# Order of the work in a slot of a fused attention and FFN kernel: P's copy and remainder first, its third block in slot 0, the last output sums in slot 3

## The chip, the core and the metric

The kernel runs on one core of a Trainium2 chip. TensorE (PE in the profile) does the matmuls, VectorE (DVE) and ScalarE (ACT) everything on elements, SyncE (SP) issues the DMAs. The metric is the device time of one execution in microseconds (us). The kernel before takes 700.49 us, the median of three runs (700.48 to 700.79).

## The reference

Eight batches of 576 tokens and 8 heads of 64 pass through an attention over 32 landmarks for each head, and the result through an FFN without bias:

```python
a = softmax(phi, axis=2)                              # 576 x 32 for each head
k_m, v_m = einsum(a, k), einsum(a, v)                 # 32 x 64 for each head
attn = softmax(q @ k_m.T / 8)                         # 576 x 32 for each head
x = (attn @ v_m).reshape(tokens, 512)
g = silu(x @ w_in)                                    # 2048 wide
out = g @ w_out                                       # 512 wide
```

All in fp32; the kernel must return the 4608 x 512 output.

## The kernel before

**Algebra.** `x @ w_in` is never formed from x: `p_mm` (line 627) multiplies v_m with w_in, which gives P (8 heads x 32 landmarks, by 2048 columns of the FFN), and `ffn1s` (line 806) multiplies attn with P. Each large matmul works on numbers that are split into a high part in a rounded type and a remainder, so three products stand for one: high x high, high x low, low x high. The names with `hi` and `lo` are these parts.

**P.** P of a batch is made in four blocks of 512 columns. A block is 16 small matmuls into the pair of PSUM banks `bg` (there is one such pair), then a copy to the high part on ACT (line 643) and the remainder on DVE (line 645, which reads `bg` and the copy). The next block can write `bg` only when line 645 is through. Blocks 0 and 1 of batch n are made in slots 13 and 14 of batch n-1, blocks 2 and 3 in slots 1 and 2 of batch n. The piece of w_in for a block is loaded anew for each batch (`win_load`, 1 MB each).

**A slot.** Batches 2 to 7 are worked in 16 slots each: t (0 or 1, half of the tokens) by j (8 groups of 256 FFN columns). A slot is written in this order: `ffn1s` makes h (12 matmuls into the one pair of banks `h`); `forms` takes SiLU of it on ACT (line 820, and line 822 for 32 columns that are kept for later), forms differences on DVE (lines 825, 828, 829) and splits the seven operands of a Winograd step into high (ACT, lines 824 and 834) and low parts (DVE, lines 835 and 836); then come the slot's *events*; then `st_step` multiplies the seven operands of the slot before with w_out (line 845, 21 matmuls into four PSUM banks `sum0` to `sum3`). In two slots of a batch (`exp_slots`) DVE makes the last four high parts instead (lines 831, 832).

**Events** are the attention of the next batches, cut into pieces and put into slots by a table (`ev(b, slot, function, arguments)`): `p_mm`; `phi_sub` (lines 310 and 313, twice each, which subtract the maxima from phi before its exp); `s_norm` (line 442), `s_back` (transposes on DVE, line 457, then a copy on ACT, line 458) and `s_low` (line 463) of the softmax of the scores; `phi_fold` (lines 284, 286, 294, 301, 302, with small DMAs between them); loads.

**Outputs.** After slots 7 and 15 the four banks hold a finished half. `st_out` copies two banks on ACT (line 878, twice), does four additions on DVE that read the other two banks (line 885), and stores two pieces; `rest`, three more additions on line 885 and two stores, is put into the list `late`, which the next slot runs ahead of its events. The next `st_step` with j = 0 writes the four banks again.

**Left-over tokens.** 64 tokens of each batch don't fit the slots. After the odd batches there are four more slots (16 to 19, "left slots") in which those of two batches go through `left_split` (ACT line 910, DVE line 911) and `left_st` (line 845, tiles `lsum`).

**What sets the order.** PE and ACT run in the order in which the code is written (`in_order`). DVE's order is set by a scheduler from priorities; `behind(i, other)` forbids it to place i ahead of `other`. In slots 0 to 15 every DVE instruction of an event (that of `s_all` excepted) is behind the last low part that `forms` wrote (`last_split`); in the left slots there is no such rule. All engines then run their queues strictly in the order that came out.

Of the kernel before, what the change touches and what calls it, by code (L numbers as in the profile page):

```python
# [16 lines left out]
ALU = mybir.AluOpType  # L17
# [8 lines left out]
NFC = DFF // P  # L26
CW = 256
JW = 512
# [20 lines left out]
def attn_ffn_kernel(  # L49
# [9 lines left out]
    nc = tc.nc  # L59
# [60 lines left out]
    raws, cvas, last_silu, last_split = {}, {}, [], []  # L120
# [480 lines left out]

    pj, wins = {}, {}
    win_saved = [hbm.tile([P, 4, NR, P], F32, name=f"win_saved{k}") for k in range(4)]

    def win_save():
# [31 lines left out]
    def p_split(b, f, w, bg, steps=(0, 1)):  # L639
        hi, lo = pj[b, f // JW]  # L640
        c = slice(f % JW, f % JW + w)
        if 0 in steps:
            nc.scalar.activation(hi[:, :, c], bg[:, :, :w], AF.Copy)
        if 1 in steps:
            nc.vector.tensor_tensor(lo[:, :, c], bg[:, :, :w], hi[:, :, c], op=ALU.subtract)  # L645

# [220 lines left out]
        if j == NP - 1:  # L869
            st_out(b, t)  # L870

    late = []

    def st_out(b, t):
        o = sb.tile([P, 2, DMODEL], F32, tag="cva", name="oo", bufs=1)
        x = sb.tile([P, 2, Q], F32, tag="cva1", name="x", bufs=1)
        for i in range(2):
            nc.scalar.activation(o[:, i], sums[i], AF.Copy)
        (c11, c21), (p3, p5) = ((o[:, i, :Q], o[:, i, Q:]) for i in range(2))
        c12, c22 = x[:, 0], x[:, 1]  # L880
        r = b * S + 2 * t * P
        one, two = slice(r + P, r + 2 * P), slice(r, r + P)

        def add(to, a, c, op=ALU.add):
            nc.vector.tensor_tensor(to, a, c, op=op)

        add(c12, sums[2][:, :Q], c11)
        add(c22, sums[2][:, Q:], c12)
        add(c11, c11, c21)
        add(c21, c22, sums[3][:, :Q], ALU.subtract)  # L890
        nc.sync.dma_start(out[one, :Q], c11)
        nc.sync.dma_start(out[two, :Q], c21)

        def rest():
            add(c22, c22, p5)
            add(c12, c12, p5)
            add(c12, c12, p3)
            nc.sync.dma_start(out[two, Q:], c22)
            nc.sync.dma_start(out[one, Q:], c12)

        late.append(rest)

    def left_split(b, n):
        flat = gparts.rearrange("p k n f -> p (k n f)")
        home = (aparts[:, 0, 1], flat, flat[:, 2 * MAIN :], aparts[:, 1, 1])[n]
        g = gleft[:, n * NI : (n + 1) * NI].rearrange("p c f -> p (c f)")
        gs = home[:, :MAIN], home[:, MAIN : 2 * MAIN]
        if b == 1:
            return split(g, gs=gs if n == 3 else None)
        nc.scalar.activation(gs[0], g, AF.Copy)  # L910
        nc.vector.tensor_tensor(gs[1], g, gs[0], op=ALU.subtract)
        return gs

    def left_st(b, n, gs):
# [23 lines left out]
    events = {}  # L938

    def ev(b, slot, fn, *a):  # L940
        events.setdefault((b, slot), []).append((fn, a))
# [39 lines left out]
    for b in range(B):  # L981
        n = b + 1
        if b == 0:
            for j in range(2, DFF // CW):
                ev(b, 2 * j - 1.5, p_mm, b, j * CW, CW)
        elif b == 1:
            ev(b, 0, win_save)
            for j in range(1, NJ):
                ev(b, 4 * j - 3, p_mm, b, j * JW, JW)
            for j in range(NP):  # L990
                ev(b, 1.5 * j + 2, w_forms, j, 0)
                ev(b, 1.5 * j + 2.5, w_forms, j, 1)
        else:
            ev(b, 0, win_load, b, 3)
            ev(b, 1, p_mm, b, 2 * JW, JW)
            if b > 2:
                ev(b, 3, s_norm, b, SECOND)
                ev(b, 4, s_back, b, SECOND)
                ev(b, 4, s_low, b, SECOND)
            ev(b, 2, p_mm, b, 3 * JW, JW)  # L1000
            if n < B:
                steady(b, n)
            continue
# [56 lines left out]
    with in_order(DVE, ACT) as last:  # L1060
# [56 lines left out]
        bg = p_mm(0, 0, CW, False)  # L1117
# [48 lines left out]
    def finish(tiles):  # L1166
# [10 lines left out]
        elif prev[0] == "st" and tiles[0] == 0:  # L1177
            st_step(*prev[1:])

    for b in range(B):  # L1180
        if b == 1:
            whole.close()
            ctx.enter_context(in_order(ACT))
        for s in range(NFC if b > 1 else 0):
            t, j = divmod(s, NP)
            h = ffn1s(b, t, j)
            part = forms(b, t, j, h)
            todo = [(fn, ()) for fn in late] + events.pop((b, s), [])
            late.clear()
            for fn, a in todo:  # L1190
                traced = nc.cur_bb.bb.instructions
                n = len(traced)
                fn(*a)
                for i in list(nc.cur_bb.bb.instructions)[n:]:
                    if i.engine == DVE and fn is not s_all:
                        behind(i, last_split[-1])
            finish(range(NI))
            prev = ("st", b, t, j, part)
        for fc in range(NFC if b < 2 else 0):
# [23 lines left out]
        if b % 2:  # L1223
            for n in range(NLS):
                gs = left_split(b, n)
                for fn, a in [(fn, ()) for fn in late] + events.pop((b, NFC + n), []):
                    fn(*a)
                late.clear()
                finish((0, 1, 2, 3))
                prev = ("left", b, n, gs)  # L1230
    finish((0,))
# [55 lines left out]
```

## Time and profile before

| | us |
|---|---|
| median of three runs | 700.49 |
| the profiled execution | 701.35 |
| its span, first to last instruction | 699.5 |
| DVE busy | 513.8 |
| ACT busy | 367.8 |

Batches 0 and 1, which go another way and are not touched, end at about 200 us of the span; batch 2 begins its slots at 200.6, batch 3 at 280.2, batch 4 at 370.6, batch 5 at 446.3, batch 6 at 536.5 and batch 7 at 612.1 us. A slot without events takes 4.1 us, one with a block of P 5.3 us.

A row of the timeline gives the start in us, the duration in us, the engine, the line, the operation, output<-inputs, the shape and the count, and in brackets how long the engine sat idle before it and what ended that. A row of the waits gives the engine and line that waited, what it waited for, the total in us, how often, and the longest. A row of the windows gives for a stretch its length and the busy time of PE, of its weight loads (PEld), DVE, ACT and POOL with their counts, then the granted TensorE clock (1.00 is full) and the DMA share.

### The profile page before, as it was taken

The page shows a single profiled execution, that of the slowest core. Times are in us where ns is not written, and L with a number is a line of the kernel's source. Part 1 is how long each engine was busy: PE and PEld are TensorE (multiplying, and loading weights), DVE is VectorE, ACT ScalarE, POOL GpSimd, SP SyncE. Part 2 cuts the span into 40 slices and gives each one's busy share as a digit, 9 for nine tenths or more (in the row PEclk, how much of TensorE's full clock was granted, in tenths as well). Part 3 has the DMA queues.
Part 4 walks back from the last instruction along what each step waited for, and adds up shares of the span by engine and source line. Part 5 has one row for each costly group of instructions (what it writes and reads, how often), then busy time and mean ns, then how long its engine had stood idle before and what let it go on. Part 6 is the DMA issues. An engine that isn't in the chain of part 4 may idle for free.

```text
span 699.5 us, 14791 instructions
## 1 busy us (share of the span) xinstructions
PE 677.5 (97%) x5932; PEld 596.8 (85%) x5932; DVE 513.8 (73%) x1084; ACT 367.8 (53%) x676; POOL 0.7 (0%) x6
## 2 busy tenths in 40 slices
PE   7999999999999998899999999989999999999997
PEld 3578777887889997799988999889989899889996
DVE  4898799788938588858874678876885567776652
ACT  3879684543535454554644546553653645554441
POOL 0000000000000000000000000000000000000000
PEclk9999999999999999999999999999999999999999
DMA  9997974324360462243420345225431204210001
GB/s 342 340 339 264 319 280 175 111 83 159 115 191 4 169 219 66 87 163 134 156 91 17 133 134 184 77 77 179 151 105 48 77 2 147 82 75 1 31 1 46
DMA packets 37749, 93.93 MB, mean 134 GB/s; under 512 B 4657, under 2 KB 21169, under 8 KB 34097
## 3 DMA queue, kind: packets, MB, share of 16 engines
q1 hardware_dynamic: 36736, 90.22, 37.4%
q10 hardware_dynamic: 944, 2.77, 1.0%
q8 instruction: 47, 0.77, 0.4%
q14 instruction: 22, 0.17, 0.1%
HBM read 77.22 MB, written 15.73 MB: 133 GB/s over the span
## 4 chain that ended last, share of the span: by engine, by line
PE 71%; DVE 8%; ACT 5%; issue 2%; DVEq 0%; ACTq 0%
PE sum L845 29%; PE h L806 18%; PE acc L705 7%; PE lsum L845 5%; PE h L664 4%; PE bg L627 3%; DVE pm L645 2%; PE accleft L705 2%; PE bg L333 1%; ACT aparts L834 1%; ACT gbuf L820 1%; DVE gbuf L825 1%; ACT L820 1%; ACT L432 1%; PE bg L380 1%
## 5 line engine op out<-in xcount | busy, mean ns | idle before, releaser
L806 PE MATMUL h<-aparts,pm 128*128 128x288 f32 x1152 | 168.9, 295 | 0.0
L806 PEld LDWEIGHTS h<-aparts,pm 128*128 128x128 f32 x1152 | 157.0, 188 | 1.0 <-issue 0.7
L820 ACT ACTIVATE gbuf<-h 128x512 f32<-128x512 f32 x96 | 57.2, 596 | 133.7 <-PE h L806 133.4
L825 DVE TENSOR_TENSOR gbuf<-gbuf 128x256 f32<-128x256 f32 x96 | 40.4, 421 | 94.3 <-ACT gbuf L820 93.8
L845 PE MATMUL sum<-wo_hi,aparts 128*128 128x256 f32 x384 | 105.1, 296 | 1.9 <-ACT aparts L834 1.8
L845 PE MATMUL sum<-wo_lo,aparts 128*128 128x256 f32 x384 | 100.4, 283 | 0.0
L845 PE MATMUL sum<-kept,aparts 128*128 128x256 f32 x576 | 100.3, 283 | 0.0
L845 PEld LDWEIGHTS sum<-wo_hi,aparts 128*128 128x128 f32 x384 | 73.1, 190 | 24.3 <-ACT gleft L822 14.2
L834 ACT ACTIVATE aparts<-gbuf 128x512 fp32r<-128x512 f32 x86 | 54.4, 633 | 67.0 <-DVE gbuf L829 67.0
L705 PE MATMUL acc<-wo_hi,gparts 128*128 128x512 f32 x256 | 86.5, 397 | 0.3 <-DVE gparts L681 0.2
L845 PEld LDWEIGHTS sum<-kept,aparts 128*128 128x128 f32 x576 | 82.8, 191 | 0.0
L845 PEld LDWEIGHTS sum<-wo_lo,aparts 128*128 128x128 f32 x384 | 73.5, 191 | 0.0
L845 PE MATMUL sum<-wo_hi,gparts 128*128 128x256 f32 x384 | 72.7, 281 | 0.0
L836 DVE TENSOR_TENSOR gparts<-gbuf,aparts 128x512 fp32r<-128x512 f32 x86 | 59.3, 690 | 18.0 <-ACT aparts L834 18.0
L845 PE MATMUL sum<-kept,gparts 128*128 128x256 f32 x288 | 65.5, 282 | 0.0
L705 PEld LDWEIGHTS acc<-wo_hi,gparts 128*128 128x128 f32 x256 | 47.7, 188 | 14.5 <-DVE t L788 1.7
L845 PEld LDWEIGHTS sum<-wo_hi,gparts 128*128 128x128 f32 x384 | 59.4, 190 | 0.0
L664 PEld LDWEIGHTS h<-aparts,pm 128*128 128x128 f32 x372 | 51.8, 188 | 7.7 <-issue 2.7
L664 PE MATMUL h<-aparts,pm 128*128 128x288 f32 x372 | 56.2, 299 | 1.3 <-DVE aparts L463 1.0
L705 PE MATMUL acc<-wo_lo,gparts 128*128 128x512 f32 x128 | 50.5, 394 | 0.8 <-DVE wo_lo L182 0.7
L824 ACT ACTIVATE aparts<-gbuf 128x384 fp32r<-128x384 f32 x96 | 50.4, 525 | 0.0
L845 PEld LDWEIGHTS sum<-kept,gparts 128*128 128x128 f32 x288 | 47.9, 190 | 0.0
(204 smaller groups left out, 986.7 us busy)
## 6 DMA issues: line engine op xcount, KB each, us to landing
win<-win_saved SPq DMA_DIRECT2D x24, 1024.0 KB, 5.0
kv<-in_kv SPq DMA_DIRECT2D x28, 516.0 KB, 4.8
q<-in_q SPq DMA_DIRECT2D x16, 576.0 KB, 5.8
raw<-in_w_in SPq DMA_DIRECT2D x14, 512.0 KB, 7.2
raw<-in_w_out SPq DMA_DIRECT2D x6, 1024.0 KB, 5.8
win_saved<-win SPq DMA_DIRECT2D x4, 1024.0 KB, 8.7
phi<-in_phi SPq DMA_DIRECT2D x7, 576.0 KB, 6.0
out<-oo SPq DMA_DIRECT2D x26, 128.0 KB, 1.8
```

The costliest lines, as they stand in the source:

```text
L333: nc.tensor.matmul(pt[p][M * r : M * (r + 1), :KVW], e[:, p, c, M * r : M * (r + 1)], kvt[c][:, p, r], start=c == 0, stop=False, skip_grou ...
L627: nc.tensor.matmul(bg[M * r : M * (r + 1), p, :w].rearrange("p (k f) -> p k f", f=P), kvT[D * p : D * (p + 1), 1, r], src[D * p : D * (p + ...
L645: nc.vector.tensor_tensor(lo[:, :, c], bg[:, :, :w], hi[:, :, c], op=ALU.subtract)
L664: nc.tensor.matmul(h[:, hf, :HALF], wt[:, p, fs], a[:, p, hf * HALF : (hf + 1) * HALF], start=n[hf] == 0, stop=n[hf] == 5, skip_group_chec ...
L705: nc.tensor.matmul(acc[key], gt[:, cs], wt[:, fc], start=fc == 0 and n == 0, stop=fc == NFC - 1 and n == 2)
L806: nc.tensor.matmul(h[:, i, :HALF], wt[:, p, f : f + P], a[:, p], start=n == 0, stop=n == 5)
L820: nc.scalar.activation(gbuf[:, :MAIN].rearrange("p (i f) -> p i f", i=2), h[:, :, :w], AF.Silu)
L824: nc.scalar.activation(hi[:, :3], g[:, 1:4], AF.Copy)
L825: nc.vector.tensor_tensor(g[:, 4:6], g[:, :1].broadcast_to([P, 2, P]), g[:, 1:3], op=ALU.subtract)
L834: nc.scalar.activation(hi[:, 3:], g[:, 4:], AF.Copy)
L836: last_split.append(nc.vector.tensor_tensor(lo[:, 3:], g[:, 4:], hi[:, 3:], op=ALU.subtract))
L845: nc.tensor.matmul(sums[bank][:, place * Q : (place + 1) * Q], gt[:, k], wt, start=bank not in begun, stop=True, skip_group_check=True,)
```

## The change

It moves work and removes or adds none:

- `run` runs the events of a slot with `p_mm` ahead of all others, and every DVE instruction of the others is kept behind the remainder of P (line 645) of that slot.
- Block 2 of P moves from slot 1 to slot 0, for batches 3 to 7.
- `rest` is now an event. For the first half it stays in slot 9, after the others. For the second half it moves to slot 3 of the next batch from slot 1 (even batches), and stays in left slot 17 after an odd one, behind `phi_sub`.
- In the left slots DVE work of events is behind the remainder of the left-over split (line 911).

```diff
-    pj, wins = {}, {}
+    pj, wins, last_p = {}, {}, []
...
         if 1 in steps:
-            nc.vector.tensor_tensor(lo[:, :, c], bg[:, :, :w], hi[:, :, c], op=ALU.subtract)
+            i = nc.vector.tensor_tensor(lo[:, :, c], bg[:, :, :w], hi[:, :, c], op=ALU.subtract)
+            last_p[:] = [i]
...
-        late.append(rest)
+        ev(*((b, 9) if t == 0 else (b, NFC + 1) if b % 2 else (b + 1, 3)), rest)
...
-        nc.vector.tensor_tensor(gs[1], g, gs[0], op=ALU.subtract)
+        last_split.append(nc.vector.tensor_tensor(gs[1], g, gs[0], op=ALU.subtract))
...
             ev(b, 0, win_load, b, 3)
-            ev(b, 1, p_mm, b, 2 * JW, JW)
+            ev(b, 0 if b > 2 else 1, p_mm, b, 2 * JW, JW)
...
+    def run(b, slot):
+        todo = events.pop((b, slot), [])
+        todo.sort(key=lambda e: e[0] is not p_mm)
+        last_p.clear()
+        for fn, a in todo:
+            n = len(nc.cur_bb.bb.instructions)
+            fn(*a)
+            for i in list(nc.cur_bb.bb.instructions)[n:]:
+                if i.engine == DVE and fn not in (p_mm, s_all):
+                    for other in [last_split[-1]] + last_p:
+                        behind(i, other)
+
...
-            todo = [(fn, ()) for fn in late] + events.pop((b, s), [])
-            late.clear()
-            for fn, a in todo:
-                traced = nc.cur_bb.bb.instructions
-                n = len(traced)
-                fn(*a)
-                for i in list(nc.cur_bb.bb.instructions)[n:]:
-                    if i.engine == DVE and fn is not s_all:
-                        behind(i, last_split[-1])
+            run(b, s)
...
-                for fn, a in [(fn, ()) for fn in late] + events.pop((b, NFC + n), []):
-                    fn(*a)
-                late.clear()
+                if b > 1:
+                    run(b, NFC + n)
```

The new lines shift the numbers: from `p_split` to `st_out` a line after is one higher than before (836 is 837), from `st_out` on one lower (885 is 884); 627, 643, 645 and all below keep theirs. The text goes by the numbers of before.

**DVE, start of batch 3.** Before, the last row of `forms` in slot 1 (line 836) is followed by `rest`, by `phi_sub` and only then by P's remainder:

```order
L836 TENSOR_TENSOR gparts<-gbuf,aparts 128x512
L885 TENSOR_TENSOR x<-x,oo 128x256 x2
L310 TENSOR_TENSOR phi_2477<-phi_2477,am 128x512
L885 TENSOR_TENSOR x<-x,oo 128x256
L313 TENSOR_TENSOR phi_2477<-phi_2477,am 64x128
L310 TENSOR_TENSOR phi_2477<-phi_2477,am 128x512
L313 TENSOR_TENSOR phi_2477<-phi_2477,am 64x128
L645 TENSOR_TENSOR pm<-bg,pm 128x1024
```

After the change the remainder stands in slot 0, directly behind `forms` and ahead of the four additions that read the banks:

```order
L837 TENSOR_TENSOR gparts<-gbuf,aparts 128x512
L645 TENSOR_TENSOR pm<-bg,pm 128x1024
L884 TENSOR_TENSOR x<-sum_2620,oo 128x256
L884 TENSOR_TENSOR x<-sum_2620,x 128x256
L884 TENSOR_TENSOR oo<-oo 128x256
L884 TENSOR_TENSOR oo<-x,sum_2621 128x256
L826 TENSOR_TENSOR gbuf<-gbuf 128x256
```

The remainder has moved up a slot; `phi_sub` alone is left in slot 1, and `rest` stands behind line 442 in slot 3. Batches 5 and 7 begin alike (7 has no `phi_sub`). At the start of batches 4 and 6, after left slots, the remainder stands ahead of the two additions of the left-over sums (lines 932, 933).

**DVE, slots 13 to 15 of batch 3.** Before, from the last row of `forms` in slot 13:

```order
L836 TENSOR_TENSOR gparts<-gbuf,aparts 128x512
L442 TENSOR_TENSOR sc_3415<-sc_3415,ssm 128x2x288
L645 TENSOR_TENSOR pm<-bg,pm 128x1024
L301 COPY wide<-fm 128x256
L825 TENSOR_TENSOR gbuf<-gbuf 128x256
L302 STREAM_TRANSPOSE am<-wide 128x256
L828 TENSOR_TENSOR gbuf<-gbuf 128x128
L310 TENSOR_TENSOR phi_3321<-phi_3321,am 128x512
L829 TENSOR_TENSOR gbuf<-gbuf 128x128
L835 TENSOR_TENSOR gparts<-gbuf,aparts 128x384
L313 TENSOR_TENSOR phi_3321<-phi_3321,am 64x128
L310 TENSOR_TENSOR phi_3321<-phi_3321,am 128x512
```

After the change:

```order
L837 TENSOR_TENSOR gparts<-gbuf,aparts 128x512
L645 TENSOR_TENSOR pm<-bg,pm 128x1024
L442 TENSOR_TENSOR sc_3415<-sc_3415,ssm 128x2x288
L301 COPY wide<-fm 128x256
L826 TENSOR_TENSOR gbuf<-gbuf 128x256
L302 STREAM_TRANSPOSE am<-wide 128x256
L829 TENSOR_TENSOR gbuf<-gbuf 128x128
L830 TENSOR_TENSOR gbuf<-gbuf 128x128
L836 TENSOR_TENSOR gparts<-gbuf,aparts 128x384
L837 TENSOR_TENSOR gparts<-gbuf,aparts 128x512
L645 TENSOR_TENSOR pm<-bg,pm 128x1024
L457 STREAM_TRANSPOSE aT_3827<-sc_3415 128x288 x2
```

Remainder and line 442 change places in slot 13; in slot 14 the remainder goes ahead of lines 457 and 463, and `phi_sub`, which the scheduler had drawn up from left slot 17 into slot 14, goes back there. Batch 5 is the same. In batches 2, 4 and 6 the remainder moves up in slots 13 and 14 alike, without a `phi_sub`.

**ACT, slot 14 of batch 3.** Before, from `forms` of slot 14 to that of slot 15:

```order
L824 ACTIVATE aparts<-gbuf 128x384
L834 ACTIVATE aparts<-gbuf 128x512
L458 ACTIVATE aparts<-aT_3815 128x2x288
L643 ACTIVATE pm<-bg 128x1024
L820 ACTIVATE gbuf<-h 128x512
```

After the change:

```order
L825 ACTIVATE aparts<-gbuf 128x384
L835 ACTIVATE aparts<-gbuf 128x512
L643 ACTIVATE pm<-bg 128x1024
L458 ACTIVATE aparts<-aT_3827 128x2x288
L821 ACTIVATE gbuf<-h 128x512
```

P's copy goes ahead of line 458, which waits for the transposes on line 457; the SiLU of slot 15 stands behind both. PE's order changes only in that block 2's 16 matmuls stand one slot earlier; on SP the two stores of `rest` go behind one load of q in slot 9 of batch 2, and behind two of kv at the start of batches 3 and 5.

More of the change, by code (lines that the diff above doesn't have):

```diff
@@ L870, in st_step @@
             st_out(b, t)
-    late = []
     def st_out(b, t):
```

## The prediction

> **What bounds the kernel now.** First the page: its span and the busy times.
>
> ```profile
> span 699.5 us, 14791 instructions
> ...
> PE 677.5 (97%) x5932; PEld 596.8 (85%) x5932; DVE 513.8 (73%) x1084; ACT 367.8 (53%) x676; POOL 0.7 (0%) x6
> ```
>
> TensorE is busy for 97% of the span. The change removes no matmul, so it can only win what TensorE waits or runs slowly. The waits of its weight loads from 200 to 700 us, where the changed slots lie, name the causes:
>
> ```profile
> PEld sum L845 <- ACT gleft L822: 14.2, 20, 0.8
> PEld bg L627 <- DVE pm L645: 8.6, 7, 2.5
> ...
> PEld sum L845 <- ACT aparts L834: 2.2, 2, 1.1
> ```
>
> The first row is the weight loads of the sums standing still while a block of P with its small weights passes: 20 times alike, and the matmuls beside them run on. The blocks stay as many, so it stays. The second is P's block waiting until the remainder of the block before has freed `bg`; the third is the sums of slot 15 waiting for their high part. In the timeline of TensorE's matmuls these waits stand one by one:
>
> ```profile
> 270.92 1.91 PE L627 MATMUL bg<-win,kvT 64*32 64x512 f32 x16 [2.28 <-DVE pm L645]
> 293.21 1.09 PE L627 MATMUL bg<-win,kvT 64*32 64x512 f32 x16 [1.88 <-DVE pm L645]
> 349.82 1.09 PE L627 MATMUL bg<-win,kvT 64*32 64x512 f32 x16 [0.27 <-DVE pm L645]
> 359.71 0.39 PE L845 MATMUL sum<-wo_hi,aparts 128*128 128x256 f32 x1 [0.88 <-ACT aparts L834]
> 438.60 0.66 PE L627 MATMUL bg<-win,kvT 64*32 64x512 f32 x8 [0.26 <-DVE pm L645]
> 459.31 0.66 PE L627 MATMUL bg<-win,kvT 64*32 64x512 f32 x8 [1.88 <-DVE pm L645]
> 515.90 0.66 PE L627 MATMUL bg<-win,kvT 64*32 64x512 f32 x8 [0.26 <-DVE pm L645]
> 525.57 0.39 PE L845 MATMUL sum<-wo_hi,aparts 128*128 128x256 f32 x1 [0.88 <-ACT aparts L834]
> 604.34 0.66 PE L627 MATMUL bg<-win,kvT 64*32 64x512 f32 x8 [0.16 <-DVE pm L645]
> ```
>
> The brackets sum to 8.75 us. They are slot 14 of batches 2 to 6, slot 2 of batches 3 and 5, and the first left slot behind batches 3 and 5. The longest has a tail, which the windows around it show (granted clock: third number from the end):
>
> ```profile
> 267.65:271.06 3.41, 1.13 (x16) 0.90 (x22) 3.18 (x6) 2.58 (x5) 0.00 (x0) 1.00 0.00 0
> ```
>
> **The change, part by part.**
>
> *Slot 2 of batches 3 and 5.* What held `bg`, in batch 3:
>
> ```profile
> 288.37 1.01 ACT L643 ACTIVATE pm<-bg 128x1024 fp32r<-128x1024 f32 x1
> ...
> 289.11 0.75 DVE L885 TENSOR_TENSOR x<-x,oo 128x256 f32<-128x256 f32 x2
> ...
> 291.93 1.22 DVE L645 TENSOR_TENSOR pm<-bg,pm 128x1024 fp32r<-128x1024 f32 x1
> ```
>
> The copy was done at 289.38, but the remainder started at 291.93, behind `rest` and `phi_sub`. Now block 2 and its remainder lie in slot 0 and `bg` is free a slot early. What can be late next is the four banks: slot 1's sums write them again, and the additions that read them now stand behind the remainder. Slot 0 and 1 as they were:
>
> ```profile
> 283.75 0.63 ACT L834 ACTIVATE aparts<-gbuf 128x512 fp32r<-128x512 f32 x1 [0.59 <-DVE gbuf L829]
> 284.29 1.06 ACT L878 ACTIVATE oo<-sum 128x512 f32<-128x512 f32 x2
> ...
> 285.03 0.42 DVE L885 TENSOR_TENSOR x<-sum,oo 128x256 f32<-128x256 f32 x1
> ...
> 286.27 0.42 DVE L885 TENSOR_TENSOR oo<-x,sum 128x256 f32<-128x256 f32 x1
> ...
> 287.00 0.39 PE L845 MATMUL sum<-wo_hi,aparts 128*128 128x256 f32 x1
> ...
> 289.59 1.74 PE L806 MATMUL h<-aparts,pm 128*128 128x288 f32 x12
> ```
>
> On ACT the copy follows line 834 (284.38) and ends 1.01 later, 285.4. The remainder takes 1.22: 286.6. The four additions take 286.69 - 285.03 = 1.66: 288.3. On TensorE the block moves ahead of slot 1's h, so slot 1's sums still begin at 287.0; 21 of them take 2.59, 0.12 each. The bank that the fourth addition frees is the last of the four to be taken up again, after ten products: 287.0 + 1.2 = 288.2. So the wait is 0.1, I take nothing; bounds 0 and 0.7 (the additions a whole 0.42 plus start-up later, or the bank taken third). Then h of slot 2 starts at 289.6 and block 3 at 291.3 in place of 293.2: 1.9 each, 3.8 for the two. Batch 7 gets the same new place and had no such wait: 0, at worst a loss of 0.7. Batches 4 and 6 follow left slots, whose sums take other banks and had no wait either: 0.
>
> *Slots 13 and 14.* In batch 2:
>
> ```profile
> 268.24 1.01 ACT L643 ACTIVATE pm<-bg 128x1024 fp32r<-128x1024 f32 x1
> 268.98 0.75 DVE L442 TENSOR_TENSOR sc<-sc,ssm 128x576 f32<-128x576 f32 x1
> 269.65 1.22 DVE L645 TENSOR_TENSOR pm<-bg,pm 128x1024 fp32r<-128x1024 f32 x1
> ...
> 275.94 0.20 DVE L294 TENSOR_REDUCE fm<-qz 32x8 f32<-32x32 f32 x1
> ...
> 280.99 0.29 DVE L301 COPY wide<-fm 128x256 f32<-128x256 f32 x1
> 281.31 0.45 DVE L302 STREAM_TRANSPOSE am<-wide 128x256 f32<-128x256 f32 x1
> ...
> 282.64 0.43 DVE L825 TENSOR_TENSOR gbuf<-gbuf 128x256 f32<-128x256 f32 x1 [0.88 <-ACT gbuf L820]
> ```
>
> Line 442's 0.75 leaves the front, but the remainder then waits for the copy (269.25): it gains 269.65 - 269.29 = 0.36, not 0.75. The gap becomes 1.9. After the 2.28 the clock fell:
>
> ```profile
> 271.07:274.47 3.40, 3.40 (x24) 1.75 (x13) 3.13 (x9) 0.63 (x1) 0.00 (x0) 0.50 0.02 1
> 289.60:293.20 3.60, 1.73 (x14) 1.50 (x12) 3.56 (x8) 1.15 (x3) 0.00 (x0) 1.00 0.21 73
> ```
>
> 3.4 us at half clock cost 1.7. The gap of 1.88 in the third stretch was not followed by it; 1.9 is nearest to that, so I expect it gone: 0.36 + 1.7 = 2.1 at the end of the batch. Little of this lasts: line 301 waits for small DMAs that start when line 294 ends, 4.85 us before it. Line 294 now stands behind the remainder and line 457 and comes some 0.3 later, so 301 and 302 end at about 282.1, and DVE's work in slot 0 of batch 3 starts there in place of 282.64. At most 0.6 gets through; with a half clock still, 0.25. I take 0.4.
>
> The Trainium skill, "TensorE: Matmul & The Clock Gate", section "Why this matters for your kernels", says that only idle gaps of more than about 3 us bring the half clock. The row of 2.28 us speaks against it; by the rule there is no half clock after the change, the term is 0.6, and the sum below 0.2 larger.
>
> In batches 4 and 6 the wait of 0.26 and 0.16 goes. In slot 14 ACT now does the copy, then waits for line 457 to do line 458, and only then the SiLU of slot 15, about 0.5 later than before: h of the next slot just gets its banks. I take 0.2 and 0.2; bounds 0 and 0.3 each.
>
> *Left slots behind batches 3 and 5.* Batch 3:
>
> ```profile
> 351.62 0.68 DVE L310 TENSOR_TENSOR phi<-phi,am 128x512 f32<-128x512 f32 x1
> ...
> 354.29 0.83 DVE L457 STREAM_TRANSPOSE aT<-sc 128x288 f32<-128x288 f32 x2
> ...
> 355.15 0.69 ACT L458 ACTIVATE aparts<-aT 128x576 fp32r<-128x576 f32 x1 [1.98 <-DVE aT L457]
> ...
> 355.87 0.76 DVE L463 TENSOR_TENSOR aparts<-aT,aparts 128x576 fp32r<-128x576 f32 x1 [0.43 <-ACT aparts L458]
> ...
> 357.93 0.41 DVE L825 TENSOR_TENSOR gbuf<-gbuf 128x256 f32<-128x256 f32 x1
> ...
> 359.03 0.63 ACT L834 ACTIVATE aparts<-gbuf 128x512 fp32r<-128x512 f32 x1 [1.23 <-DVE gbuf L829]
> ```
>
> `phi_sub` (two of 0.68, two of 0.28) leaves slot 14. Line 829 then follows 828 at 351.6 (line 310's start), 834 ends at 352.6, the copy at 353.5, the remainder at 354.8, the transposes (0.83) at 355.6, line 458 at 356.3 and 463 (0.76) at 357.1. So line 825 of slot 15 starts at 357.0, 0.9 early, and so does 834, on which the sums wait. They stood 0.88 + 0.27 and more, so 0.9 gets through: 1.8 for both batches. `phi_sub` then lies in left slots that are TensorE's alone; in them line 911 comes up to 1.9 later, with some 0.5 to spare before its product.
>
> *Stores.* `rest`'s two stores now queue behind loads that wait for TensorE; no later tile needs their space before slot 4: 0.
>
> Sum: 3.8 + 0.4 + 0.2 + 0.2 + 1.8 = 6.4 us. The profiled execution took 701.35 (span 699.5 and 1.85 around it): 694.95. The three timed runs have a median 0.86 below it; if that is a fixed difference, 694.1, if it is the half clock (0.86 of its 1.7), 694.95 stands. I say **694.5**.
>
> **Rivals.**
>
> *The wait moves to the banks.* The additions come late for slot 1's sums in batches 3, 5, 7: 0.7 each, 2.1 in all, **696.6**. For: by my times the margin is 0.1. Against: the last bank is needed last.
>
> *The left slots give nothing,* since the SiLU of slot 15 stays behind line 458: 694.5 + 1.8 = **696.3**. For: ACT's order. Against: the working above.
>
> *The change does not do what it says.* The order shows it done; what could fail is that each freed wait is taken up at once by another on DVE, which is busy for 93% and 99% of the windows that hold the gaps (3.18 of 3.41; 3.56 of 3.60). Then **700.5**.
>
> *Slower: the remainder blocks DVE's queue.* At the head of DVE in slots 13, 14 and 0 it waits for the copy, and the next `forms` stand behind it. That a queue's head holds the rest is seen here: line 301 waited for a DMA and line 825, whose input was there, ran behind it.
>
> ```profile
> 350.54 0.29 DVE L301 COPY wide<-fm 128x256 f32<-128x256 f32 x1 [0.78 <-DMA fm<-fm]
> ```
>
> The same page of the Trainium skill, section "Architectural detail", calls ACT and DVE strict FIFO; the row agrees. The price is the lateness of `forms` beyond its slack: line 836 of slot 0 ended at 285.1 and its products come at 287.0 + 1.7, so 3.6. In three slots of five batches, to lose the 6.4 and 1.5 more, it must be 0.5 beyond that each time, 4.1 in all, where I find under 1: **702**.
>
> **How the numbers follow.** Forecast 0.59 (693.2 to 695.9), banks 0.20, left slots 0.09, no change 0.07, slower 0.05. A measurement tells 0.2% (1.4 us) from no change. So faster 0.88, same 0.07, slower 0.05. The range 692.9 to 697.4 holds the first three cases and their bounds.
>
> **What would show it.** Right: no bracket over 0.1 at slot 2 of batches 3 and 5; line 834 of slot 15 about 0.9 earlier against its h; the granted clock 1.00 throughout batch 2; none of the sums in slot 1 waiting for line 885. Wrong: a bracket "DVE x" or "oo" at those sums, a bracket at h naming line 822 after slot 14, or line 825 late behind the remainder.

## The result, and the profile after

| | before | after |
|---|---|---|
| median, us | 700.49 (699.12 to 700.79, 4 runs) | 693.74 (693.05 to 694.86, 4 runs) |
| ratio to before, 95% interval | | 0.9909 (0.9889 to 0.9929) |
| profiled execution | 701.35 | 693.13 |
| its span | 699.5 | 691.3 |

The change is faster by 0.9%. The forecast of 694.5 with the range 692.9 to 697.4 held. How it came to hold is less simple than the number: one term of the sum was five times too small, and part of what it is made of, a stretch of half clock, comes in some executions and not in others. In all that follows one profiled execution, that of the kernel phi11 (below), was slow throughout (1662.55 us, where its three others took 692.15 to 693.08), and nothing is read from its trace.

From here on rows of the kernels after the change have its line numbers: 834 and 845 of before are 835 and 846, and 885 is 884. The page of after, span and busy times:

```profile
span 691.3 us, 14788 instructions
...
PE 676.0 (98%) x5932; PEld 596.3 (86%) x5932; DVE 515.1 (75%) x1084; ACT 367.4 (53%) x676; POOL 0.7 (0%) x6
```

The waits of TensorE's matmuls from 200 us on, where before had the nine rows at lines 627 and 845 that the prediction quotes (each row: what waited for what, the total, how often, the longest):

```profile
PE bg L627 <- DVE pm L645: 1.9, 1, 1.9
PE sum L846 <- ACT aparts L835: 0.6, 2, 0.4
PE h L380 <- ACT gleft L823: 0.3, 1, 0.3
```

One wait for `bg` is left (batch 2, slot 14), and the two of the left slots have shrunk from 0.88 to 0.42 and 0.20. The third row is not new: before it was 0.2. A wait that PE's records show is only a part of what a stage loses, so the table gives the lengths themselves: from the first h matmul of a slot to the first of the next, worked out from the start times of lines 806 and 807.

| us | before | after | less | forecast |
|---|---|---|---|---|
| slot 2, batch 3 and 5 | 7.25, 7.23 | 5.28, 5.29 | 3.9 | 3.8 |
| slot 14 of batch 2 | 9.23 | 7.28 | 1.95 | 0.4 |
| slot 14, batches 4 and 6 | 5.64, 5.54 | 5.31, 5.31 | 0.6 | 0.4 |
| slot 14 to the left slots' end, batch 3 and 5 | 22.80, 22.57 | 21.75, 21.38 | 2.25 | 1.8 |
| all other places | | | -0.5 | 0 |
| sum | | | 8.2 | 6.4 |

8.2 is the difference of the two spans. The losses of the last row are 0.2 in slots 0 and 1 of batch 5, 0.16 in slots 5 and 6 of batch 2, and 0.1 in slot 15 of batch 4.

The timeline of ACT and DVE in slot 0 and 1 of batch 3 after the change, and the first of the rows of P's block 3 in slot 2:

```profile
282.44 1.00 ACT L643 ACTIVATE pm<-bg 128x1024 fp32r<-128x1024 f32 x1
283.35 1.08 ACT L877 ACTIVATE oo<-sum 128x512 f32<-128x512 f32 x2
...
283.48 1.23 DVE L645 TENSOR_TENSOR pm<-bg,pm 128x1024 fp32r<-128x1024 f32 x1 [0.22 <-ACT pm L643]
284.62 0.41 DVE L884 TENSOR_TENSOR x<-sum,oo 128x256 f32<-128x256 f32 x1
...
285.86 0.42 DVE L884 TENSOR_TENSOR oo<-x,sum 128x256 f32<-128x256 f32 x1
...
289.41 0.66 PE L627 MATMUL bg<-win,kvT 64*32 64x512 f32 x8
```

The remainder waits for nothing but the copy and ends at 284.71; block 3 comes 4.7 us later and has no bracket. The fourth addition ends at 286.28. Slot 1's sums began at 285.24, and ten products of 0.12 later, at 286.44, its bank is taken up, if it is the last of the four as the prediction has it: it is free 0.16 early.

Batch 2, slots 13 to 15 on DVE, and its block of P on PE:

```profile
269.35 1.22 DVE L645 TENSOR_TENSOR pm<-bg,pm 128x1024 fp32r<-128x1024 f32 x1 [0.22 <-ACT pm L643]
...
270.63 0.67 PE L627 MATMUL bg<-win,kvT 64*32 64x512 f32 x8 [1.90 <-DVE pm L645]
...
276.26 0.16 DVE L294 TENSOR_REDUCE fm<-qz 32x8 f32<-32x32 f32 x1
...
279.53 0.69 DVE L837 TENSOR_TENSOR gparts<-gbuf,aparts 128x512 fp32r<-128x512 f32 x1 [0.23 <-ACT aparts L835]
280.14 0.29 DVE L301 COPY wide<-fm 128x256 f32<-128x256 f32 x1
...
280.83 0.39 DVE L826 TENSOR_TENSOR gbuf<-gbuf 128x256 f32<-128x256 f32 x1
```

The wait of 1.90 is the 1.9 that was forecast. Line 301 starts right behind line 837, without a bracket, 3.72 behind the end of line 294. DVE's work of slot 0 of batch 3 (line 826) begins at 280.83, where line 825 began at 282.64 before. Before, line 301 had no bracket either, and the forms ahead of it had themselves been waiting for the SiLU of slot 15:

```profile
278.60 0.42 DVE L825 TENSOR_TENSOR gbuf<-gbuf 128x256 f32<-128x256 f32 x1 [1.19 <-ACT gbuf L820]
...
280.38 0.69 DVE L836 TENSOR_TENSOR gparts<-gbuf,aparts 128x512 fp32r<-128x512 f32 x1 [0.23 <-ACT aparts L834]
280.99 0.29 DVE L301 COPY wide<-fm 128x256 f32<-128x256 f32 x1
```

What line 301 reads was there by then. The view of the tile `fm` before, from 275 to 283 us, has the three small DMAs that write it (first and last issue, then the time from issue to landing):

```profile
L88 SPq DMA_DIRECT2D fm<-fm x3: 507/588/591, 276.2 to 277.4; - x3
...
DMA to landing us min/median/max: 1.7/1.7/1.7
```

The last landed at about 277.4 + 1.7 = 279.1, 1.9 before line 301 began.

The first left slot behind batch 3:

```profile
353.06 0.42 DVE L826 TENSOR_TENSOR gbuf<-gbuf 128x256 f32<-128x256 f32 x1
...
354.17 0.63 ACT L835 ACTIVATE aparts<-gbuf 128x512 fp32r<-128x512 f32 x1 [0.77 <-DVE gbuf L830]
...
354.85 0.39 PE L846 MATMUL sum<-wo_hi,aparts 128*128 128x256 f32 x1 [0.42 <-ACT aparts L835]
```

Slot 15's h started at 349.29 here and at 353.44 before, so line 835 starts 4.88 behind it where line 834 started 5.59 behind it: 0.71 earlier, not 0.9.

### The profile page after: what moved, and what is told of

It is laid out like the page before. It is cut to its first block, busy times and chain, and to the rows that moved or that the text cites. A ratio compares the mean times of both kernels' runs of the same rounds, so it can differ in the third digit from the quotient of the medians.

```text
span 691.3 us, 14788 instructions
## 1 busy us (share of the span) xinstructions
PE 676.0 (98%) x5932; PEld 596.3 (86%) x5932; DVE 515.1 (75%) x1084; ACT 367.4 (53%) x676; POOL 0.7 (0%) x6
## 4 chain that ended last, share of the span: by engine, by line
PE 75%; DVE 6%; ACT 3%; issue 1%; DMA 1%; SPq 0%; DVEq 0%; ACTq 0%
PE sum L846 31%; PE h L807 20%; PE acc L706 7%; PE lsum L846 5%; PE h L665 4%; PE bg L627 3%; PE accleft L706 2%; PE bg L333 1%; DVE pm L645 1%; PE bg L380 1%; ACT pm L643 1%; DMA fm<-fm 1%; DVE gbuf L826 0%; ACT gbuf L821 0%; DVE aT L457 0%
```

## The experiments

Each is the changed kernel with one or more parts undone or moved, timed beside the kernel before, on three chips (before: 700.96, 700.88 and 700.60). The questions were: which of the parts frees `bg` in slot 2; whether the left slots' rule is worth anything; what the order inside a slot is worth; and what the half clock in batch 2 hangs on. All results together, stage lengths as above (a star: the profiled execution had 3.4 us of half clock in that slot):

| | median, us | ratio (95%) | span | slot 14, batch 2 | slot 2, batch 3 / 5 | slot 3, batch 3 / 5 | slot 14 to left slots' end, batch 3 / 5 |
|---|---|---|---|---|---|---|---|
| before | 700.49 | | 699.5 | 9.23* | 7.25 / 7.23 | 5.30 / 5.30 | 22.80 / 22.57 |
| after | 693.74 | 0.9909 (0.9889 to 0.9929) | 691.3 | 7.28 | 5.28 / 5.29 | 5.30 / 5.30 | 21.75 / 21.38 |
| after_again | 693.47 | 0.9895 (0.9871 to 0.9919) | 691.6 | 7.32 | 5.28 / 5.29 | 5.30 / 5.30 | 21.83 / 21.39 |
| blk1 | 693.49 | 0.9887 (0.9866 to 0.9908) | 692.2 | 8.80* | 5.29 / 5.29 | 5.30 / 5.30 | 21.64 / 21.39 |
| rest1 | 695.21 | 0.9913 (0.9895 to 0.9931) | 694.0 | 8.81* | 5.29 / 5.29 | 5.93 / 5.98 | 21.85 / 21.39 |
| blk1_rest1 | 695.89 | 0.9917 (0.9895 to 0.9939) | 694.5 | 8.84* | 5.29 / 5.29 | 6.07 / 6.11 | 21.93 / 21.41 |
| nosort | 694.90 | 0.9904 (0.9886 to 0.9923) | 692.1 | 9.18* | 5.29 / 5.28 | 5.30 / 5.30 | 21.31 / 21.31 |
| nosort_blk1 | 696.67 | 0.9937 (0.9914 to 0.9960) | 693.7 | 7.68 | 6.24 / 6.24 | 5.30 / 5.30 | 21.74 / 21.32 |
| left_old | 694.96 | 0.9906 (0.9886 to 0.9925) | 693.5 | 8.80* | 5.29 / 5.29 | 5.30 / 5.30 | 22.29 / 22.03 |
| s14 | 694.49 | 0.9901 (0.9881 to 0.9921) | 692.4 | 8.83* | 5.29 / 5.28 | 5.30 / 5.30 | 21.66 / 21.34 |
| phi11_s14 | 691.95 | 0.9869 (0.9846 to 0.9892) | 690.4 | 6.54 | 5.29 / 5.28 | 5.30 / 5.30 | 21.79 / 21.35 |
| best | 691.33 | 0.9866 (0.9842 to 0.9889) | 689.5 | 6.32 | 5.29 / 5.29 | 5.30 / 5.30 | 21.17 / 21.17 |

The starred spans are some 1.5 us longer than the same kernel's would be without the half clock (worked out below), so across stars the stages are to be compared, not the spans; the medians are of executions with and without it.

### Block 2 of P back in slot 1 (blk1)

```diff
-            ev(b, 0 if b > 2 else 1, p_mm, b, 2 * JW, JW)
+            ev(b, 1, p_mm, b, 2 * JW, JW)
```

> Block 2 of P back in slot 1, all else as after the change. Theory A (what frees bg in time is that the remainder stands ahead of phi_sub and rest; the slot of the block doesn't matter): the remainder starts when the copy ends, about 2.5 us earlier than before, and block 3 in slot 2 of batches 3 and 5 finds bg free. No wait of block 3 over 0.1, span within 0.4 of the 691.3 after the change (in executions with equal clock). Theory B (the move into slot 0 does it): 1.9 us come back in batches 3 and 5 each, span about 695.1.

Theory A holds. ACT and DVE in slot 1 of batch 3, and block 3:

```profile
287.60 1.01 ACT L643 ACTIVATE pm<-bg 128x1024 fp32r<-128x1024 f32 x1
288.64 1.23 DVE L645 TENSOR_TENSOR pm<-bg,pm 128x1024 fp32r<-128x1024 f32 x1 [0.22 <-ACT pm L643]
289.78 0.68 DVE L310 TENSOR_TENSOR phi<-phi,am 128x512 f32<-128x512 f32 x1
...
290.49 1.09 PE L627 MATMUL bg<-win,kvT 64*32 64x512 f32 x16
```

The remainder ends at 289.87, 0.6 before block 3 begins, and the median is that of the change. So the headline of the change, the block in slot 0, is not needed for the 3.8; with the new order inside the slot it is worth nothing that can be measured.

### The output sums back in slot 1 (rest1, and blk1_rest1 with both back)

```diff
-        ev(*((b, 9) if t == 0 else (b, NFC + 1) if b % 2 else (b + 1, 3)), rest)
+        ev(*((b, 9) if t == 0 else (b, NFC + 1) if b % 2 else (b + 1, 1)), rest)
```

> rest of the second half back in slot 1 (from slot 3) for batches 3, 5 and 7, block 2 stays in slot 0. Theory A (rest was harmful only because it stood ahead of a remainder): slot 1 has no remainder any more, so only forms of slot 2 can be late: DVE ended phi_sub at 290.36 and line 826 of slot 2 started at 290.39, so rest's 1.1 us push it, and h of slot 3 loses up to 0.5 in batches 3 and 5: span 691.3 to 692.3. Theory B (moving rest was needed for the gain of slot 2): a wait of 1 us or more of block 3 in slot 2, span over 693.

> Block 2 back in slot 1 and rest back in slot 1, behind P's remainder and phi_sub; the order inside a slot and the left slots stay as after. Theory A (the order inside the slot alone frees bg for block 3; the two moves only spread DVE's work): no wait of block 3 in slot 2 over 0.1, but forms of slot 2 come 1.2 us later than with block 2 in slot 0 and rest in slot 1, so its remainder is late for the attention's matmuls on bg in slot 3, which waited 0.73 and 0.78 there: 1.5 to 2 each in batches 3 and 5; span 693 to 695.5. Theory B (with rest in slot 1 the waits of before are back): 1.9 in slot 2 of batches 3 and 5.

No wait comes back in slot 2 in either, so theory B falls in both. But the work is late one slot further on. The timeline of rest1 in slots 1 to 3 of batch 3:

```profile
291.41 0.29 DVE L313 TENSOR_TENSOR phi<-phi,am 64x128 f32<-64x128 f32 x1
291.73 0.76 DVE L884 TENSOR_TENSOR x<-x,oo 128x256 f32<-128x256 f32 x2
...
295.37 1.22 DVE L645 TENSOR_TENSOR pm<-bg,pm 128x1024 fp32r<-128x1024 f32 x1
296.69 1.09 PE L333 MATMUL bg<-kv,phi 128*32 128x129 f32 x32 [0.57 <-issue]
```

`rest` behind `phi_sub` pushes the forms of slot 2, these push the remainder of block 3 (it ends at 296.59), and the attention's matmuls on `bg` in slot 3 start 0.1 later. The bracket says "issue", but the wait is for this remainder; batch 5 has the like with "DVE pm L645" in the list of waits. Slot 3 grew by 0.63 and 0.68; with block 2 in slot 1 as well by 0.77 and 0.81. The first expectation, up to 0.5 each, was a little low, the second, 1.5 to 2, twice too high: I had added the delays of two slots. With block 2 in slot 1 the forms of that slot end earlier (line 837 starts at 288.00 in blk1_rest1, at 289.31 in rest1), which makes room for its remainder: line 826 of slot 2 starts at 292.54 there and at 292.41 in rest1.

### The order inside the slot undone (nosort, and nosort_blk1 with the block back in slot 1)

```diff
-        todo.sort(key=lambda e: e[0] is not p_mm)
+        todo.sort(key=lambda e: e[0].__name__ != "rest")
...
-                    for other in [last_split[-1]] + last_p:
+                    for other in [last_split[-1]]:
```

> Events in the order in which they are written, P's block last, with no rule that keeps other DVE work behind its remainder; block 2 in slot 0, rest in slot 3 and the left slots stay as after. Theory A: slot 14 of batches 3 to 6 waits 0.2 to 0.4 again each (1.2 in all), batch 2's wait of 1.9 becomes 2.3, slot 2 stays free; span 692.9, and 1.7 more with a half clock in batch 2. Theory B (the order inside the slot is what frees bg in slot 2 as well): waits of 1 us or more in slot 2 of batches 3 and 5, span 695 or more. In all four kernels batch 2 keeps a wait of 1.9 or more: if the half clock comes in some executions of the same program and not in others, the runs of each kernel lie in two groups some 1.5 us apart with clocks 0.998 and 0.996; if it is tied to the length of the wait alone, the first three kernels never show it and nosort always does.

> Of the change only rest in slot 3 and the left slots' rule are kept: block 2 in slot 1, events in the order in which they are written, so that the remainder in slot 1 stands behind phi_sub but no longer behind rest. Theory A (each of the two, rest and phi_sub, gives its own part of the 1.88 us wait in slot 2): rest's three additions of 0.42 are gone from ahead of it, phi_sub's 1.9 stay: the wait of block 3 in batches 3 and 5 falls from 1.88 to 0.7 to 0.9; span 1.4 to 1.8 above the 692.1 to 693.5 of the same kernel with block 2 in slot 0. Theory B (rest alone made the wait): under 0.2.

With the block in slot 0, slot 2 stays free without the order (5.29): there is no other DVE event in slot 0 to stand ahead of the remainder. With the block in slot 1 the wait is back by half. DVE of nosort_blk1 in slot 1 of batch 3, and block 3:

```profile
287.57 0.68 DVE L310 TENSOR_TENSOR phi<-phi,am 128x512 f32<-128x512 f32 x1
...
289.39 1.22 DVE L645 TENSOR_TENSOR pm<-bg,pm 128x1024 fp32r<-128x1024 f32 x1
...
290.67 1.09 PE L627 MATMUL bg<-win,kvT 64*32 64x512 f32 x16 [0.87 <-DVE pm L645]
```

0.87 of the 1.88 stays: that is `phi_sub`'s part, and the missing 1.0 was that of `rest` (theory A in both kernels). So block 3 has two cures, either of which is enough: the block in slot 0, or its remainder ahead in slot 1.

In slot 14 nosort is as expected, 0.35, 0.36, 0.35 and 0.25 longer in batches 3 to 6 than after. What was not expected is that its left slots are shorter than the change's: 21.31 in both batches from slot 14 to their end, with the 0.35 already in it. From slot 15 on that is 0.79 and 0.41 less. With a half clock its span is 692.1 where 694.6 was expected.

The slots that the table of the result calls "all other places" lose nothing in nosort either: slots 0 and 1 of batch 5, 5 and 6 of batch 2 and 15 of batch 4 take 9.38, 9.40 and 4.12, as before (9.37, 9.40, 4.12; after 9.57, 9.56, 4.23). Outside slot 14 of batch 2, where the wait is 2.3 in place of 1.9, the kernel without the order is in sum 0.4 shorter: what the order wins in slot 14 of batches 3 to 6, 1.3, comes back elsewhere.

### The left slots' rule undone (left_old)

```diff
-                if b > 1:
-                    run(b, NFC + n)
+                for fn, a in sorted(events.pop((b, NFC + n), []), key=lambda e: e[0].__name__ != "rest"):
+                    fn(*a)
```

> Left slots run their events as before the change: no rule that puts them behind line 910, so phi_sub lies in slot 14 of batches 3 and 5 again; all else as after. Theory A (my term of 1.8): line 835 of slot 15 comes 0.7 to 0.9 later again in both batches and the first left slot waits for it, span 691.3 + 1.4 to 1.8 = 692.7 to 693.1. Theory B (the rival: the left slots gain nothing from it, and what they won came from P's remainder going first): span 691.3 to 691.6.

`phi_sub` is back in slot 14, and the stretch to the left slots' end is 22.29 and 22.03, 0.54 and 0.65 longer than after: 1.2 us, so theory B falls, and A's 1.4 to 1.8 was a little too high. The other 1.05 of the 2.25 is what the rest of the change brings without the rule. The two do not add up, for the rule without the order inside the slot brings all of it: from slot 14 to the left slots' end, nosort is 1.49 and 1.26 shorter than before and nosort_blk1 1.06 and 1.25.

### P's block last in slot 14 alone (s14)

```diff
-        todo.sort(key=lambda e: e[0] is not p_mm)
+        if slot != 14:
+            todo.sort(key=lambda e: e[0] is not p_mm)
```

> P's block goes first in every slot but slot 14, where it goes behind lines 457, 458 and 463 as before the change; all else as after. Theory A (slot 14's wait for bg is decided by the order in slot 13 alone, and P's copy ahead of line 458 in slot 14 delays the SiLU of slot 15): slot 14 stays at 5.3 us in batches 3 to 6, the first left slot's wait (0.58 and 0.36) goes and slot 15 with its left slots takes 15.65 in place of 16.44 and 16.07: 1.2 us less than the change, span 690.1 without and 691.7 with a half clock in batch 2. Theory B (slot 14 needs its own block first): slot 14 back at 5.65, 1.4 lost for 1.2 won, span 691.5 and 693.1.

Half of theory A holds. Slot 14 stays at 5.31, so its wait is made in slot 13. The left slots win nothing (21.66 and 21.34), so ACT's order in slot 14 is not what holds them. DVE of s14 from slot 13 to slot 15 shows what does:

```profile
345.70 1.23 DVE L645 TENSOR_TENSOR pm<-bg,pm 128x1024 fp32r<-128x1024 f32 x1 [0.22 <-ACT pm L643]
...
347.87 0.29 DVE L301 COPY wide<-fm 128x256 f32<-128x256 f32 x1 [0.27 <-DMA fm<-fm]
...
356.08 0.39 PE L846 MATMUL sum<-wo_hi,aparts 128*128 128x256 f32 x1 [0.47 <-ACT aparts L835]
```

With the remainder first DVE stands still for 0.22 until the copy is there, and for 0.27 until line 301's DMA is; in nosort, whose line 442 fills the first of the two, neither row has a bracket. From line 837 of slot 13 to line 826 of slot 15 DVE takes 9.51 (344.79 to 354.30) here and 9.17 (344.53 to 353.70) in nosort, and the first left slot waits 0.47 here and not at all there. Of the two stops it is the second that costs. nosort_blk1, which has no order inside the slot either, stops there for longer:

```profile
347.90 0.29 DVE L301 COPY wide<-fm 128x256 f32<-128x256 f32 x1 [0.66 <-DMA fm<-fm]
```

It takes 9.58 for the same stretch (344.74 to 354.32), and its left slots end 21.74 behind the start of slot 14, as late as the change's. The change in batch 5 has the 0.22 and no stop at line 301, and takes 9.24 (506.53 to 515.77); nosort takes 9.17 there too (507.23 to 516.40). So the copy's 0.22 costs 0.07, and 0.66 at line 301 costs 0.41. Why line 301's DMAs are in time in nosort and not in nosort_blk1 stays open.

s14 also shows the rival of the late banks: in batch 3 the fourth addition ends at 287.61, slot 1's eleventh product comes at 287.67, where the spacing of those before it gives 287.46, and slots 0 and 1 take 9.71 in place of 9.38.

### What is left in batch 2 (phi11, phi11_s14, best)

```diff
-            ev(b, 7 if early else 12, phi_max, m)
+            ev(b, 7 if early else 11, phi_max, m)
             for i in range(3):
-                ev(b, 11 + i if early else 13 + i, phi_fold, m, i, load)
+                ev(b, 11 + i if early else 12 + i, phi_fold, m, i, load)
```

> In batch 2 the maxima of phi (lines 256 to 259) go from slot 12 to slot 11 and the three steps behind them one slot earlier, all else as after the change. Theory A (the wait of 1.9 us in slot 14 of batch 2 is left because lines 256 to 259 and 284, 2.1 us in all, stand among the forms of slot 13, and this wait is what lets the half clock come in some executions): wait under 0.4, no half clock there in any run; against executions of the change without a half clock (span 691.3) 1.6 to 1.9 less, so spans of 689.3 to 689.8 in all runs but for what the last microseconds do; median time about 691.5. Theory B (the wait comes from line 436, which stays): wait over 1.2 us, two groups of runs 1.5 apart as before.

> Both of the two other changes together (phi's maxima of batch 2 a slot earlier; slot 14 with P's block last). If both theories A hold and the two don't touch each other: 691.3 - 1.8 - 1.2 = 688.3 for the span in all runs, median time about 690.2. If one of them takes up what the other frees: 689.5 or more.

The three timed runs of phi11 gave 692.15, 692.43 and 693.08, with spans of 690.3 to 691.3 where theory A had 689.3 to 689.8; it stands in no table. phi11_s14 shows the wait: 1.16 where under 0.4 was expected. So the maxima were worth 0.7 of the 1.9; lines 284 and 286 stand among the forms of slot 13 now, and lines 436 to 438 still do, the longest of which (436) theory B named. Neither theory holds alone. The span of phi11_s14, 690.4, is not the 688.3 of two gains that add up; s14 by itself had brought none.

The last kernel moves both folds that were left in the way:

```diff
-            ev(b, 7 if early else 12, phi_max, m)
-            for i in range(3):
-                ev(b, 11 + i if early else 13 + i, phi_fold, m, i, load)
+            ev(b, 7 if early else 11, phi_max, m)
+            for i, at_ in enumerate((11, 12, NFC if b % 2 else 13) if early else (11, 13, 14)):
+                ev(b, at_, phi_fold, m, i, load)
```

> All as after the change, but phi's maxima and the first fold of batch 2 go to slot 11 (lines 256 to 259, 284, 286), the last fold of batches 3 and 5 (lines 301, 302) from slot 13 to left slot 16. Theory A (what is left in slot 14 of batch 2 and in the first left slots is DVE's work between slot 12 and slot 15, and DVE has idle time in slots 11 and 16): the wait in slot 14 of batch 2 under 0.4 (1.9 after the change, 1.2 with the maxima alone moved), the first left slots' 0.58 and 0.36 under 0.1, no half clock in any run: span 691.3 - 1.7 - 0.9 = 688.7 in all runs, give or take 0.5, median time about 690.5. Theory B (the waits are set by ACT's order and DMAs): 690 or more.

The waits of best from 195 us on:

```profile
PE bg L627 <- DVE pm L645: 0.9, 1, 0.9
PE h L380 <- ACT gleft L823: 0.2, 1, 0.2
```

The left slots wait for nothing: lines 301 and 302, one of the two stops and 0.7 us of DVE's work ahead of slot 15, held them. Batch 2 still waits 0.9, where under 0.4 was expected; of the work in question lines 436 to 438 (1.34, 0.18 and 0.37) are what still stands among the forms of slot 13. The span of 689.5 is longer than theory A's 688.7, give or take 0.5, and shorter than theory B's 690. The median is 691.33, the fastest of all here: 2.1 below the change's 693.47 on the same chip.

### The half clock

> The change itself again, beside the others on the same chip. If the half clock behind the wait of 1.9 us in batch 2 is a matter of the execution: spans in two groups, 691 and 692.6 to 693, as in its first four runs (two and two). If those were a matter of the chip: one group.

Its six spans were 691.2, 691.3, 691.6, 691.7, 691.9 and 692.5: hardly two groups, where the first four runs had 691.3 twice, 692.6 and 693.0; the times decide neither. The profiles say more. A window in each of five kernels is the stretch of 3.41 us that the clock's own records mark off there (these records change only at whole multiples of 3.413 us from one another: in before, 78 of them lie between the first full clock and the half clock). Before, slot 2 of batch 3:

```profile
291.54:294.96 3.42, 1.75 (x22) 0.91 (x23) 3.07 (x8) 1.53 (x4) 0.00 (x0) 1.00 0.11 38
```

blk1, batch 2, and the stretch behind it:

```profile
267.48:270.89 3.41, 1.50 (x23) 0.76 (x21) 2.96 (x5) 2.45 (x5) 0.00 (x0) 1.00 0.00 0
270.89:274.31 3.42, 3.42 (x21) 2.81 (x14) 2.94 (x8) 1.54 (x2) 0.00 (x0) 0.50 0.01 1
```

After, the same place:

```profile
269.00:272.42 3.42, 1.79 (x22) 0.96 (x23) 3.20 (x7) 1.36 (x4) 0.00 (x0) 1.00 0.00 0
272.42:275.83 3.41, 3.41 (x29) 3.41 (x28) 2.92 (x6) 1.55 (x2) 0.00 (x0) 1.00 0.03 1
```

nosort, and nosort_blk1, both with a wait of 2.3:

```profile
267.79:271.21 3.42, 1.12 (x17) 0.18 (x16) 3.42 (x7) 1.77 (x4) 0.00 (x0) 1.00 0.00 0
271.21:274.62 3.41, 3.41 (x24) 3.40 (x17) 2.40 (x7) 1.43 (x3) 0.00 (x0) 0.50 0.03 1
```

```profile
266.84:270.25 3.41, 1.81 (x14) 1.57 (x12) 3.13 (x8) 2.52 (x5) 0.00 (x0) 1.00 0.18 72
270.25:273.67 3.42, 2.73 (x30) 1.89 (x31) 3.15 (x8) 0.69 (x2) 0.00 (x0) 1.00 0.01 0
```

The first number behind the length is PE's busy time. Where the wait lies whole inside one such stretch, PE is busy for 1.1 to 1.5 of its 3.41 us and the next stretch runs at half clock; where the stretch's edge cuts the wait, or takes in less of it, PE is busy for 1.7 us or more and the clock stays. So it is in all ten profiles with a wait of 1.9 or more there: seven had 1.12 to 1.51 and the half clock, three had 1.67 to 1.81 and none. The length of the wait decides only whether it can happen: 2.3 us went with and without. In best, where it is 0.9, the stretch is busy for 2.48. The end of each kernel, where TensorE has nothing more to do, agrees. There the last stretch with work was busy for 1.55 us in rest1 and was not followed by the half clock, for 1.50 in left_old and was:

```profile
687.54:690.96 3.42, 1.55 (x13) 1.35 (x12) 0.76 (x2) 0.38 (x1) 0.00 (x0) 1.00 0.00 0
690.96:694.00 3.04, 0.00 (x0) 0.00 (x0) 0.00 (x0) 0.00 (x0) 0.00 (x0) 1.00 0.33 86
```

```profile
687.17:690.59 3.42, 1.50 (x13) 1.29 (x11) 0.76 (x2) 0.38 (x1) 0.00 (x0) 1.00 0.00 0
690.60:693.50 2.90, 0.00 (x0) 0.00 (x0) 0.00 (x0) 0.00 (x0) 0.00 (x0) 0.50 0.34 90
```

In all the whole stretches of the twelve profiles that the table lists, from the first full clock on, none with 1.55 or more was followed by the half clock, and each with 1.51 or less was. In batch 2 the half clock cost 1.5 us (8.80 to 8.84 against 7.28 and 7.32 at the same wait of 1.9; 9.18 against 7.68 at 2.3).

## Why the prediction was right, and where it was not

**Slot 2, 3.8: right, for the reason that was given, with one addition.** 3.9 came, and the rival "banks" stayed small: 0.16 to spare in batch 3. In batch 5 the fourth addition ended at 449.36, and the sum that began at 449.43 took 0.09 longer than its neighbours (0.37 for 0.28), which fits that rival's mechanism at an eighth of its price. The addition is that two edits were each enough for it.

**Batch 2, 0.4: the step that failed is the cap.** What the prediction worked out first, 0.36 + 1.7 = 2.1 at the end of the batch, came as 1.95 in slot 14. It then read line 301 as held by its DMAs, 4.85 us behind line 294, and let only 0.6 through. But the row of line 301 had no bracket: it stood behind line 836 in DVE's queue, and its DMAs had landed about 1.9 earlier. After the change it comes 3.72 behind line 294's end, again straight behind the forms. With no floor at 4.85 the whole 1.95 went through to batch 3. The reading would have been right one batch on: in batches 3 to 5 of before line 301 starts 5.07, 5.43 and 4.84 behind line 294 with brackets of 0.78, 1.14 and 0.56 that name the DMA, and the landing takes 3.3 to 5.1 there.

**The half clock: the conclusion fitted the profiled run, the reasoning did not.** I argued from the length of the wait, since 1.88 in slot 2 went without and 2.28 in slot 14 with a half clock. Neither length decides: blk1 had the same wait of 1.9 as the change and fell to half clock. The change leaves a wait of 1.9, and with it the half clock in some executions. The Trainium skill, "TensorE: Matmul & The Clock Gate", section "Part 1: The HAM clock gate (the "warmup" mystery)", has such a free-running window of about 3.4 us; the ten profiles agree with that. The rule in its section "Why this matters for your kernels", that gaps over about 3 us are to be avoided, falls short here: a wait of 1.9 us had a half clock behind it.

**Slot 14 of batches 4 and 6, 0.4:** 0.6 came; the delay of the SiLU that I set against it cost 0.1 in batch 4 (slot 15 takes 4.23, in s14, where line 458 is ahead again, 4.12 as before) and nothing in batch 6.

**Left slots, 1.8:** 2.25 came, and `phi_sub`'s move, which the term named, is enough for all of it: without the order it brings 2.3 (nosort_blk1) or 2.75 (nosort), and on top of the order 1.2 (left_old). In batch 3 line 834 of slot 15 came 0.71 earlier and not 0.9; DVE still waits there for line 301's DMA, for 0.31.

**Sum.** Against the profiled execution of before, which had a half clock, the profiled execution of after, which had none in the batches (only behind the last matmul), is 8.2 shorter; 6.4 was forecast. The medians differ by 6.75: two of the four runs after the change, 694.34 and 694.86, lie 1.2 to 1.8 above the other two at a mean granted clock of 0.997 and 0.996 (0.998 and 0.999), which fits a half clock; these two have no trace. That the forecast of 694.5 lies only 0.8 from the median is in part luck: the median lies between executions with and without the half clock, and the two fastest, 693.05 and 693.13, are 0.15 and 0.23 inside the range. The kernel before is mixed in the same way. In the 33 executions of it that were timed beside the experiments the span runs from 697.1 at a mean granted clock of 1.000 to 702.2 at 0.992. One stretch of 3.41 us at half clock lowers the mean by 0.0024, so an estimate from these numbers gives the slowest two or three such stretches, and before had three waits of 1.88 or more: slot 14 of batch 2 and slot 2 of batches 3 and 5. These executions have no trace, so it is not shown that the change also took half clocks out of slot 2.

**Rivals.** No change and slower are out by the interval. That the remainder blocks DVE's queue did happen, for 0.22 a time, at a price of 0.07 where it could be told apart (batch 5, under s14). The 0.5 lost in "all other places" is absent in both kernels without the order: 0.1 of it is the SiLU above, 0.09 the banks, and what makes the rest stays open. That the left slots give nothing is refuted by left_old.

## What to carry to other kernels

When one engine frees a buffer for another, look first at what stands ahead of the freeing instruction in its own queue: taking other work out from in front of it was worth as much here as making the buffer's content a slot earlier, and either alone was enough. A floor such as "this waits for a DMA" needs the bracket that names the DMA; a long time between two rows without one is only a place in a queue. And an instruction that waits at the head of its engine's queue holds back all that stands behind it; the price is to be measured, as 0.22 for the copy cost 0.07 here and 0.66 for the DMA of line 301 cost 0.41.

## What the runs showed of the hardware

An idle gap of TensorE of 1.9 us between dense matmuls brought 3.4 us of half clock in seven of ten profiles with a gap of 1.9 to 2.3 us at one place, and none in the others, by how the gap lay against stretches of 3.413 us: PE busy 1.51 us or less of one brought it, 1.67 or more did not; at the kernels' ends 1.50 did and 1.55 did not. Between dense matmuls it cost 1.5 us. With the wait at 0.9 the runs of best lie between 691.14 and 691.80, where those of the change reach from 692.96 to 694.86.
